# Stationary columns of the row-maximum matmuls in an LSH attention and gMLP kernel: step four against step two in the long phase

## The chip, the cores and the metric

The kernel runs on one core of a Trainium2 chip. The metric is the device time of one execution in microseconds (us); less is better. Of the kernel before there are three timed runs, and one more execution that was profiled.

## The reference

Attention with hashed buckets, for 4 batches of 8 heads, 768 positions and 64 values per head, and behind it a gated MLP on the joined heads:

```python
q_bits = (np.einsum('bhsd,dk->bhsk', q, proj) > 0)      # 6 bits make a bucket; k_bits alike
mask = q_bucket[:, :, :, None] == k_bucket[:, :, None, :]
scores = np.where(mask, scale * np.matmul(q, k.transpose(0, 1, 3, 2)), -1e9)
scores = scores - np.max(scores, axis=-1, keepdims=True)
attn = np.exp(scores)
attn = attn / (np.sum(attn, axis=-1, keepdims=True) + 1e-09)
x = np.matmul(attn, v)              # heads joined: (4, 768, 512)
h = gelu(x @ w_in); u, v = halves of h; v_n = layer norm of v
v_s = np.einsum('ts,bsd->btd', w_sg, v_n) + b_sg[None, :, None]
return x + (u * v_s) @ w_out
```

## The kernel before, in words

**Attention.** Two heads of a batch make a pair; there are 16 pairs (NPAIR). The two heads lie on partitions 0 to 63 and 64 to 127 (`row(j)`, j = 0 and 1), so most matmuls come in twos that use the two halves of the array's rows. Per pair the kernel loads q, k and v, transposes q and k on TensorE (L512), splits them into a rounded part `h` and a rest `l`, and builds a feature tile `f` (L532 and L537) whose product with itself is zero where the buckets agree and a huge negative number where not. Row MROW of each half of `f` is spare: the negated row maximum of each query is written there, so that the same product also takes the maximum away.

The 768 query columns are worked in two phases, `PHASES = ((0, 256), (256, 768))`: a short one of 256 columns (two tiles of 128 queries) and a long one of 512 columns (four tiles).

*Maxima* (`largest`, L542 to 570). A pair has 9 units, u = 0 to 8, three for each two query tiles: u = 0 to 2 belong to the short phase, 3 to 8 to the long one. In a unit 128 query columns are the weights (the stationary operand, loaded by a LDWEIGHTS) and key columns stream against them. Units with w = 0 or 1 stream 512 key columns against one query tile: 4 matmuls (f and h, two heads each). Units with w = 2 (u = 2, 5 and 8) stream the last 256 key columns against two query tiles: 8 matmuls of 256 columns. VectorE (DVE) takes the maximum of each result (L566, L568). The two results of a unit hold two PSUM slots out of seven until DVE has read them.

A query tile is not 128 neighbouring columns. Column q0 + i0 + t + step * p is query p of tile i0 + t, with step 2 in the short phase and 4 in the long one; so the weights of the long phase are read with a step of four FP32 values, those of the short phase with a step of two.

*Shift* (`shift`, L572 to 587). Behind u = 2 and u = 8 a last reduction on DVE (L576) makes `m`, 128 partitions x (head, tile), and two DMAs (L584, one per head) carry it into row MROW of `f`. With step 4 the four values of a partition are four neighbouring columns, so one DMA of 128 pieces of 16 bytes fills all 512 columns; in the short phase the pieces have 8 bytes. The DMAs are issued by SyncE (SP), for the first pair by ScalarE (ACT). SP works its queue in order.

*Weighing* (`weigh`, L589 to 639). Per unit 16 matmuls against h, l and f (L609), with contiguous key columns as weights, exp on ACT (L614), sums over units on GpSimd (POOL, L636), and products with v (L627 short, L624 long). The first three matmul steps of a unit do not read `f`; the fourth does, and it needs the shift. `finish` (L643 to 684) adds up the sums (L658), sends them through DRAM (s, sq, r, rs: five DMAs) and writes the pair's result to `xs`.

**MLP**, per batch: `hidden` (L826, L854), `gate` (L872), `project` (L898), with weights split by DVE, ACT and POOL (`weight_job`).

**The order** is written by a planner (`Plan.order`): each group of instructions has an engine, an assumed cost, a priority (smaller is sooner) and what it reads and writes. The planner plays all engines forward with those costs and emits every engine's instructions in the order that comes out. The assumed cost of a maxima unit is 0.45 us for w below 2 and 0.48 us for w = 2, in both phases; of a POOL add 1.29 us. On TensorE a group of another form (row, col, full, c32) ranks STAY later than its priority. Weigh unit c of pair n has priority 2 * (9 n + c); maxima unit u runs AHEAD = 8 units earlier, at S0P behind that; SHIFTP is added to it for the shift; FINP is the offset of `finish`, WP that of the attention's share of weight jobs; FIRSTS and LATE space the first pairs; MLP["wg"], ["wo"] and ["x"] are the priorities of the gate weights, the output weights and the next batch's loads. A DMA with `lat` keeps its queue busy for its cost, and what it writes is due SHIFTL = 3.2 us after its start.

Of the kernel before, what the change touches and what calls it, by code (L numbers as in the profile page):

```python
# [9 lines left out]
F32 = mybir.dt.float32  # L10
# [8 lines left out]
DRAM = bass.MemoryType.DRAM  # L19


MLP = {"xl": "POOL", "gm": "DVE", "gl": "POOL", "wg": 79.89, "wo": 101.06, "x": 735.35}

AVP = 5.16
GY, GX, NPT = (1, 2), (3, 3), 16
NAV = 1
S0P = 0.64
AHEAD = 8
PREP, SHIFTP, FINP, WSTEP, WP = -3.11, 0.54, 2.09, 14.6, 13.23
LOADS = "SP"  # L30
ADDS = (["POOL", "POOL"], ["POOL", "POOL", "POOL", "POOL", "POOL"])
TAILP = 0.59
FIRSTP, FIRSTS, FIRSTQ, LATE = 1.7, 0.42, -5.0, 5.94
WHURRY = 20.0
JOBBANK = False
AHEAD1 = 0.14
# [1 line left out]
SHIFTL = 3.2  # L38


class Plan:
# [8 lines left out]
    TURNS = {"row": 0.2, "col": 0.144, "full": 0.17, "c32": 0.1, None: 0.0}  # L50
    LANES = 8
    TURN = 4.7
    STAY = 3.9

    class Buf:
        def __init__(self, make, i, prev, need=None):
# [54 lines left out]
    def order(self):  # L111
# [13 lines left out]
        free, seq, ready, dma_free, pe, till, lanes = {}, {}, {}, 0.0, {}, {}, []  # L125
# [8 lines left out]
        def when(n):  # L134

            return max([at[n]] + [sorted(b.slots.values())[i] for i, b in enumerate(wants[n])])
# [7 lines left out]
        while len(out) < len(G):  # L144

            first = {}
            for e, rs in ready.items():
                ws = [n for n in rs if wants[n]]
                if len(ws) > 1:
                    t = min(max(when(n), since(n)) for n in rs)  # L150
                    m = min((n for n in ws if max(at[n], since(n)) <= t + 1e-9), key=lambda n: (G[n]["p"], n), default=None)
                    if m is not None:
                        first[e] = m

            def early(n):
                e = G[n]["e"]
                return not wants[n] or e not in first or first[e] == n

            t0, e = min((max(when(n), since(n)), e) for e, rs in ready.items() for n in rs if early(n))
            if t0 > 1e8:  # L160
                raise RuntimeError("no slot becomes free")
            def rank(n):
                return G[n]["p"] + (self.STAY if e == "PE" and G[n]["form"] != form else 0.0), n

            n = min((n for n in ready[e] if early(n) and max(when(n), since(n)) <= t0 + 1e-9), key=rank)
            g = G[n]
            soon = [m for m in ready[e] if early(m) and max(when(m), since(m)) <= t0 + self.SOON * g["c"] and rank(m) < rank(n)]
            if soon:
                n = min(soon, key=rank)
                g = G[n]  # L170
            ready[e].remove(n)
            start = max(t0, when(n), since(n))
            cost = g["c"]
            if e == "PE":

                work = g["c"] + (self.TURNS[g["form"]] if g["form"] != form else 0.0)
                form = g["form"]
                at_, cost = start, 0.0
                while work > 1e-9:

                    k = int(at_ / self.TICK + 1e-9)
                    slow = 2.0 if pe.get(k - 1, 0.0) < self.WARM * self.TICK else 1.0
                    t = min(work * slow, (k + 1) * self.TICK - at_)
                    pe[k] = pe.get(k, 0.0) + t / slow
                    work, at_, cost = work - t / slow, at_ + t, cost + t
            end, seq[e] = start + cost, start
            if g["dma"] and g["c"] > 1 and not g["lat"]:
                end = dma_free = max(dma_free, start + 0.6) + self.TURN
                seq[e] = max(start + 3.6, end - 1.5)
                end += 0.3  # L190
                lanes.append(end + self.WAIT)
            elif g["lat"]:

                seq[e], end = end, start + g["lat"]
                lanes.extend([end + self.WAIT] * (2 if g["c"] > 1 else 1))
            elif g["dma"]:
                seq[e] = end
                end = dma_free = max(dma_free, start + (1.38 if e == "ACT" else 1.3 if g["c"] > 1 else 1.2)) + g["dma"]
                end += 0.75
                lanes.append(end + self.WAIT)  # L200
            else:
                free[e] = end
                if g["port"]:
                    port = end
            out.append((start, n))
            at_end[n] = end
            for b in wants[n]:
                b.i = min(b.slots, key=b.slots.get)
                b.slots[b.i] = 1e9
            for b in g["slots"]:  # L210
                left[b] -= 1
                till[b] = max(till.get(b, 0), end)
                if not left[b]:
                    b.slots[b.i] = till[b] + self.WAIT
            for m in users[n]:
                need[m] -= 1
                if n in G[m]["deps"]:
                    at[m] = max(at[m], end if G[m]["e"] == e and not g["dma"] else end + self.WAIT)
                else:
                    at[m] = max(at[m], start)  # L220
                if not need[m]:
                    ready[G[m]["e"]].append(m)
# [12 lines left out]
def kernel(  # L235
# [19 lines left out]
    P = 128  # L255
# [42 lines left out]
    BL, MROW = 64, 0  # L298
# [94 lines left out]
    PE, DVE, ACT, POOL, SP = "PE", "DVE", "ACT", "POOL", "SP"  # L393
    xs = [[dram.tile([P, S], F32, name=f"xs_{b}_{hp}") for hp in range(NP)] for b in range(B)]

    plan = Plan()
# [45 lines left out]
    if True:  # L442
# [30 lines left out]
        def row(j):  # L473
            return slice(j * D, (j + 1) * D)

        def two(t):
            return t[:, :WIDE].rearrange("p (a b) -> p a b", a=2)
# [64 lines left out]
        def largest(st, u, prio):  # L542

            ph = 0 if u < 3 else 1
            i, w = divmod(u - 3 * ph, 3)
            if u in (0, 3):
                st.mx = plan.buf("mx", 3, lambda i: mxs[i % 3])
            mx, sc, i0 = st.mx, [ps_tile() for j in range(2)], 2 * i
            (a, b), (q0, q1) = ((0, WIDE) if w < 2 else (WIDE, S)), PHASES[ph]
            step = (q1 - q0) // P  # L550
            tiles = (w,) if w < 2 else (0, 1)

            def mm():
                for c, t in enumerate(tiles):
                    qs = slice(q0 + i0 + t, q1, step)
                    for n, x in enumerate((st.ft, st.hi)):
                        for j in range(2):
                            nc.tensor.matmul(sc[j]()[:, c * NY:c * NY + b - a], x()[row(j), 0, qs], x()[row(j), 1, a:b],  # L558
                                             start=(n == 0), stop=(n == 1))

            plan.add(PE, 0.45 if w < 2 else 0.48, prio, mm, [(x, (0, ph)) for x in (st.hi, st.ft)] + [(x, (1, c)) for x in (st.hi, st.ft) for c in ((0, 1) if w < 2 else (1,))],
                     sc, form="row")
            for j in range(2):
                def top(j=j):
                    if w < 2:
                        nc.vector.tensor_reduce(mx()[:, 0, i0 + w, j:j + 1], sc[j]()[:, :WIDE], axis=AX.X, op=ALU.max, negate=True)  # L566
                    else:
                        nc.vector.tensor_reduce(mx()[:, 1, i0:i0 + 2, j], two(sc[j]()), axis=AX.X, op=ALU.max, negate=True)  # L568

                plan.add(DVE, 0.69, prio, top, [sc[j]], [(mx, (u, j))])  # L570

        def shift(st, ph, prio):  # L572

            mx, m = st.mx, late.ring([P, 2, WIDE // P], F32R, "m", 3)
            nt = (PHASES[ph][1] - PHASES[ph][0]) // P
            plan.add(DVE, 0.18, prio, lambda: nc.vector.tensor_reduce(  # L576
                m()[:, :, :nt], mx()[:, :, :nt].rearrange("p a i j -> p j i a"), axis=AX.X, op=ALU.min), [mx], [m])
            ft, cs = st.ft, slice(*PHASES[ph])

            def carry():  # L580
                eng = nc.scalar if st.n == 0 else nc.sync
                for j in range(2):
                    r = j * BL + MROW
                    eng.dma_start(ft()[r:r + 1, 0, cs].bitcast(F32).rearrange("a (p t) -> a p t", t=nt),  # L584
                                  m()[:, j, :nt].bitcast(F32))

            plan.add(ACT if st.n == 0 else SP, 1.14, prio, carry, [m], [(ft, (0, ph))], dma=0.1, lat=SHIFTL)

        def weigh(st, c, prio):  # L589

# [108 lines left out]
        def maxima(i, p0=None):  # L699
# [3 lines left out]
            if p0 is None:  # L703
                p0 = 2 * (i - AHEAD) + S0P
            largest(sts[n], u, p0)
# [6 lines left out]
        for n in range(NPAIR):  # L712
            for c in range(NU):
                if c == 0:
                    prepare(n + 1)
                g = NU * n + c
# [8 lines left out]

    M_ = MLP
    end = even.close(early.close())
    b1 = Pool("b1", "right", None, end)
    end = odd.close(end)
    b2 = Pool("b2", "right", None, end)  # L730
    end = late.close(end)
    b3 = Pool("b3", "right", None, end)
    end = ps_s.close()
    pm = Pool("pm", "right", PSUM, end)
    end = ps_t.close(end)
# [176 lines left out]
    for b in range(B):  # L912
        p = 500 + 1000 * b
        h = hidden(b, xx, p)
# [40 lines left out]
```

## Time and profile before

| | us |
|---|---|
| median of 3 runs | 782.47 |
| lowest and highest | 781.77, 783.87 |
| the profiled execution | 784.53 |
| its span, first to last instruction | 782.7 |
| TensorE busy in the span | 766.3 (98%) |
| VectorE, ScalarE, GpSimd busy | 487.1, 330.0, 398.8 |
| granted TensorE clock, mean | 0.993 of full |

The profiled execution's own time is 784.53 us: 1.8 us lie around its span, and it is 2.06 us (0.26%) above the median. Attention takes the first 460 us, the MLP the rest; a pair takes some 27 us. Matmuls overlap, and the ends that the trace gives are modelled, so for TensorE starts are read rather than durations.

### The profile page before, as it was taken

The page shows a single profiled execution, that of the slowest core. Times are in us where ns is not written, and L with a number is a line of the kernel's source. Part 1 is how long each engine was busy: PE and PEld are TensorE (multiplying, and loading weights), DVE is VectorE, ACT ScalarE, POOL GpSimd, SP SyncE. Part 2 cuts the span into 40 slices and gives each one's busy share as a digit, 9 for nine tenths or more (in the row PEclk, how much of TensorE's full clock was granted, in tenths as well). Part 3 has the DMA queues.
Part 4 walks back from the last instruction along what each step waited for, and adds up shares of the span by engine and source line. Part 5 has one row for each costly group of instructions (what it writes and reads, how often), then busy time and mean ns, then how long its engine had stood idle before and what let it go on. Part 6 is the DMA issues. An engine that isn't in the chain of part 4 may idle for free.

```text
span 782.7 us, 14498 instructions
## 1 busy us (share of the span) xinstructions
PE 766.3 (98%) x5512; PEld 606.6 (78%) x5512; DVE 487.1 (62%) x899; ACT 330.0 (42%) x639; POOL 398.8 (51%) x366
## 2 busy tenths in 40 slices
PE   5999999999999999999999989999999999999998
PEld 4767767667676766767677549998899889988996
DVE  5897787878877899987977318688314061306130
ACT  1355555646455564545546634513332143113211
POOL 0276686768768677776877972442125023402030
PEclk9999999999999999999999989999999999999999
DMA  5223333243323323332322245411321401050003
GB/s 121 56 62 72 74 99 90 60 102 90 83 72 103 90 65 84 90 96 69 90 56 57 65 133 161 147 34 37 118 83 42 157 6 41 0 159 4 1 1 134
DMA packets 107749, 60.72 MB, mean 78 GB/s; under 512 B 73888, under 2 KB 94496, under 8 KB 107680
## 3 DMA queue, kind: packets, MB, share of 16 engines
q1 hardware_dynamic: 103840, 56.65, 26.8%
q10 hardware_dynamic: 3840, 3.16, 1.3%
q8 instruction: 43, 0.70, 0.4%
q14 instruction: 26, 0.21, 0.1%
HBM read 46.90 MB, written 12.78 MB: 76 GB/s over the span
## 4 chain that ended last, share of the span: by engine, by line
PE 94%; POOL 1%; issue 1%; DMA 1%; DVE 1%; ACTq 0%; ACT 0%; SPq 0%; POOLq 0%
PE g L609 17%; PE ps_vs L872 13%; PE g L558 10%; PE av L624 10%; PE ps_h L826 9%; PE ps_h L854 9%; PE ps_o L898 8%; PE av L627 5%; PE g L532 5%; PE g L512 3%; PE g L658 2%; PE ps_o L903 1%; POOL sum L636 1%; DMA k<-in_k_dram 1%; PE ps_h L792 1%
## 5 line engine op out<-in xcount | busy, mean ns | idle before, releaser
L636 POOL TENSOR_TENSOR sum<-sum,p 128x512 f32<-128x512 f32 x160 | 190.7, 1221 | 49.3 <-ACT p L614 49.2
L614 ACT ACTIVATE p<-g 128x512 f32<-128x512 f32 x288 | 157.7, 598 | 128.9 <-PE g L609 128.0
L566 DVE TENSOR_REDUCE mx<-g 128x1 f32<-128x512 f32 x192 | 123.4, 682 | 33.9 <-PE g L558 31.0
L636 POOL TENSOR_TENSOR sum<-p,p 128x512 f32<-128x512 f32 x64 | 83.1, 1320 | 90.9 <-ACT p L614 90.9
L624 PE MATMUL av<-p,v 128*64 128x512 f32 x384 | 89.0, 600 | 0.0
L875 DVE SCALAR_TENSOR_TENSOR gt<-ps_vs,g_col,b_bc 128x384 f32<-128x384 f32 x32 | 19.7, 616 | 92.7 <-PE ps_vs L872 90.9
L558 PE MATMUL g<-f 64*128 64x512 f32 (+1 forms) x384 | 77.0, 386 | 0.3 <-DVE mx L566 0.3
L558 PE MATMUL g<-h 64*128 64x512 f32 (+1 forms) x384 | 74.3, 373 | 0.0
L609 PE MATMUL g<-h 64*128 64x256 f32 (+1 forms) x384 | 71.6, 354 | 0.1
L883 POOL TENSOR_TENSOR gs<-gt,gs 128x384 fp32r<-128x384 f32 x32 | 32.6, 1018 | 74.9 <-ACT gs L880 74.9
L568 DVE TENSOR_REDUCE mx<-g 128x2 f32<-128x512 f32 x96 | 61.8, 683 | 13.1 <-PE g L558 12.3
L558 PEld LDWEIGHTS g<-f 64*128 64x128 f32 x384 | 55.8, 271 | 16.9 <-issue 10.3
L609 PE MATMUL g<-h,l 64*128 64x256 f32 (+1 forms) x384 | 68.4, 338 | 0.0
L609 PE MATMUL g<-f 64*128 64x256 f32 (+1 forms) x384 | 68.1, 337 | 0.0
L609 PE MATMUL g<-l,h 64*128 64x256 f32 (+1 forms) x384 | 67.8, 335 | 0.0
L898 PE MATMUL ps_o<-woh,gs 128*128 128x512 f32 x192 | 65.5, 402 | 0.0
L872 PE MATMUL ps_vs<-wgh,zh 128*128 128x384 f32 x192 | 64.1, 334 | 0.0
L872 PE MATMUL ps_vs<-wgh,zl 128*128 128x384 f32 x192 | 64.1, 334 | 0.0
L872 PE MATMUL ps_vs<-wgl,zh 128*128 128x384 f32 x192 | 64.1, 334 | 0.0
L624 PEld LDWEIGHTS av<-p,v 128*64 128x64 f32 x384 | 24.9, 136 | 46.0 <-issue 45.3
L837 POOL TENSOR_TENSOR mv<-mv,epsr 128x1 f32<-128x1 f32 x24 | 15.7, 656 | 87.6 <-DVE mv L836 87.6
L761 POOL TENSOR_TENSOR xl<-x,xh 128x768 fp32r<-128x768 f32 x16 | 29.9, 1883 | 55.1 <-ACT xh L763 55.0
(115 smaller groups left out, 1630.8 us busy)
## 6 DMA issues: line engine op xcount, KB each, us to landing
q<-in_q_dram SPq DMA_DIRECT2D x32, 192.0 KB, 3.6
v<-in_v_dram SPq DMA_DIRECT2D x16, 384.0 KB, 3.3
x<-xs SPq DMA_DIRECT2D x16, 384.0 KB, 3.0
rx<-xs SPq DMA_DIRECT2D x96, 64.0 KB, 2.0
out_dram<-ob SPq DMA_DIRECT2D x24, 256.0 KB, 2.2
k<-in_k_dram SPq DMA_DIRECT2D x30, 192.0 KB, 3.2
w<-in_moe_w_in_dram SPq DMA_DIRECT2D x16, 256.0 KB, 3.5
rs<-r SPq DMA_DIRECT2D x32, 128.0 KB, 3.0
```

The lines of the kernel that those rows point to most:

```text
L532: nc.tensor.matmul(fp()[:, c * n:(c + 1) * n], w[:, s, :], x()[:, s, cs], start=(u == 0), stop=(u == 2))
L558: nc.tensor.matmul(sc[j]()[:, c * NY:c * NY + b - a], x()[row(j), 0, qs], x()[row(j), 1, a:b], start=(n == 0), stop=(n == 1))
L566: nc.vector.tensor_reduce(mx()[:, 0, i0 + w, j:j + 1], sc[j]()[:, :WIDE], axis=AX.X, op=ALU.max, negate=True)
L568: nc.vector.tensor_reduce(mx()[:, 1, i0:i0 + 2, j], two(sc[j]()), axis=AX.X, op=ALU.max, negate=True)
L609: nc.tensor.matmul(sc[j]()[:, i * w:(i + 1) * w], x()[row(j), 1, ks], y()[row(j), 0, cs], start=(m == 0), stop=(m == 3))
L614: plan.add(ACT, 0.6, prio, lambda j=j: nc.scalar.activation(p[j]()[:, :, :NY], two(sc[j]()), AF.Exp, scale=SCALE), [sc[j]], [p[j]])
L624: nc.tensor.matmul(two(av())[row(j)], st.v()[:, j, x, :], ps[x][j]()[:, :, :NY], start=(x == 0), stop=(x == 5))
L636: (nc.gpsimd if e == POOL else nc.vector).tensor_add(two(sums[j]()), a, p[j]()[:, :, :NY])
L826: nc.tensor.matmul(ps(), x()[:, ts_], w[:, c, FH:FF], start=(c == 0 and n == 0), stop=(c == NC - 1 and n == 2))
L854: nc.tensor.matmul(ps()[:, :SH], w[:, c, fs], x()[:, cs], start=(c == 0 and n == 0), stop=(c == NC - 1 and n == 2))
L872: nc.tensor.matmul(vp(), z()[:, t, fs], w()[:, t, cs], start=(t == 0 and n == 0), stop=(t == NT - 1 and n == 2))
L898: nc.tensor.matmul(po(), a()[:, ts_], w()[:, f, :], start=(f == 0 and n == 0), stop=False)
```

## The change

The weights of a query tile in the long phase step over two columns instead of four: each two tiles (i0 and i0 + 1) share a block of 256 columns and alternate in it. The short phase is as it was. So that the maxima still reach their columns, the shift of the long phase goes in four DMAs instead of two: for each block of 256 columns and each head one DMA of 128 pieces of 8 bytes. The short phase's shift stays at two. The planner is told of the longer issue (0.57 us per DMA) and of four DMAs in flight. Ten planner numbers change as well.

```diff
-MLP = {"xl": "POOL", "gm": "DVE", "gl": "POOL", "wg": 79.89, "wo": 101.06, "x": 735.35}
+MLP = {"xl": "POOL", "gm": "DVE", "gl": "POOL", "wg": 72.25, "wo": 104.87, "x": 755.39}
-S0P = 0.64
+S0P = 0.66
-PREP, SHIFTP, FINP, WSTEP, WP = -3.11, 0.54, 2.09, 14.6, 13.23
+PREP, SHIFTP, FINP, WSTEP, WP = -3.11, 1.68, 0.2, 14.6, 14.91
-FIRSTP, FIRSTS, FIRSTQ, LATE = 1.7, 0.42, -5.0, 5.94
+FIRSTP, FIRSTS, FIRSTQ, LATE = 1.7, 0.26, -5.0, 5.43
-    STAY = 3.9
+    STAY = 4.85
...
-                lanes.extend([end + self.WAIT] * (2 if g["c"] > 1 else 1))
+                lanes.extend([end + self.WAIT] * max(1, round(g["c"] / 0.57)))
...
-            step = (q1 - q0) // P
...
-                    qs = slice(q0 + i0 + t, q1, step)
+                    qs = slice(q0 + i0 * P + t, q0 + (i0 + 2) * P, 2)
...
-                for j in range(2):
-                    r = j * BL + MROW
-                    eng.dma_start(ft()[r:r + 1, 0, cs].bitcast(F32).rearrange("a (p t) -> a p t", t=nt),
-                                  m()[:, j, :nt].bitcast(F32))
-
-            plan.add(ACT if st.n == 0 else SP, 1.14, prio, carry, [m], [(ft, (0, ph))], dma=0.1, lat=SHIFTL)
+                for h in range(0, nt, 2):
+                    hs = slice(cs.start + h * P, cs.start + (h + 2) * P)
+                    for j in range(2):
+                        r = j * BL + MROW
+                        eng.dma_start(ft()[r:r + 1, 0, hs].bitcast(F32).rearrange("a (p t) -> a p t", t=2),
+                                      m()[:, j, h:h + 2].bitcast(F32))
+
+            plan.add(ACT if st.n == 0 else SP, 0.57 * nt, prio, carry, [m], [(ft, (0, ph))], dma=0.1, lat=SHIFTL)
```

## Rows read from the trace of the kernel before

**Rows 1.** Busy time of TensorE, VectorE, ScalarE and GpSimd in three stretches (the attention's steady part, the handover to the MLP, the MLP); columns: stretch, its length, then busy us and instructions of each engine, granted clock, DMA share and GB/s.
```profile
27.00:430.00 403.00, 402.92 (x3548) 286.08 (x3548) 335.50 (x565) 213.49 (x427) 288.41 (x249) 1.00 0.32 80
430.00:460.50 30.50, 26.67 (x198) 13.68 (x199) 8.33 (x17) 15.92 (x32) 28.62 (x25) 0.98 0.27 76
460.50:782.70 322.20, 318.58 (x1663) 291.44 (x1663) 126.17 (x256) 95.13 (x173) 80.76 (x80) 0.99 0.23 73
```

**Rows 2.** Waits of TensorE's matmuls over the whole span, all there are: who waited for whom, us in total, times, longest.
```profile
PE g L512 <- DMA q<-in_q_dram: 3.3, 1, 3.3
PE g L512 <- DMA k<-in_k_dram: 3.2, 1, 3.2
PE ps_h L826 <- POOL xl L761: 2.5, 2, 2.0
PE ftp L431 <- DVE frow L328: 2.1, 1, 2.1
PE g L658 <- POOL sum L636: 1.3, 2, 0.8
PE g L558 <- DVE mx L566: 0.3, 1, 0.3
```

**Rows 3.** Weight loads by group, whole span: line, engine, operation, tiles, shape, count, busy us, mean ns of one, idle time before.
```profile
L558 PEld LDWEIGHTS g<-h 64*128 64x128 f32 x384 | 56.1, 274 | 0.5
...
L609 PEld LDWEIGHTS g<-h,l 64*128 64x128 f32 x384 | 38.8, 187 | 2.8
```

**Rows 4.** The maxima's line in two short stretches: 327.0 to 328.3 us, which holds one w = 2 unit of the long phase, and 333.9 to 336.2 us, which holds a w = 1 and a w = 2 unit of the short phase; durations in ns, least, median and most.
```profile
L558 PEld LDWEIGHTS g<-h x4: 326/326/326, 327.3 to 327.9; 64*128 64x128 f32 x4
...
L558 PEld LDWEIGHTS g<-h x6: 190/194/195, 334.1 to 335.7; 64*128 64x128 f32 x6
```

**Rows 5.** TensorE's instructions in order of time: start, us, what, count. First the four steps of a w = 2 unit of the long phase and the step behind them, then the same of the short phase.
```profile
53.21 0.39 PE L558 MATMUL g<-f 64*128 64x256 f32 x2
53.44 0.40 PE L558 MATMUL g<-h 64*128 64x256 f32 x2
53.67 0.40 PE L558 MATMUL g<-f 64*128 64x256 f32 x2
53.91 0.40 PE L558 MATMUL g<-h 64*128 64x256 f32 x2
54.14 0.28 PE L609 MATMUL g<-h 64*128 64x256 f32 x2
...
335.50 0.28 PE L558 MATMUL g<-f 64*128 64x256 f32 x2
335.62 0.28 PE L558 MATMUL g<-h 64*128 64x256 f32 x2
335.74 0.28 PE L558 MATMUL g<-f 64*128 64x256 f32 x2
335.86 0.28 PE L558 MATMUL g<-h 64*128 64x256 f32 x2
```

**Rows 6.** The chain of work that ended last, one pair's stretch from 409 us on: start, us, what, count. An x8 of L558 is a w = 2 unit, an x4 one of the others.
```profile
409.06 0.93 PE g L558 x8
...
410.95 0.46 PE g L558 x4
...
415.66 0.69 PE g L558 x4
...
417.27 0.47 PE g L558 x8
...
422.32 0.78 PE g L558 x4
...
425.43 0.82 PE g L558 x8
```

**Rows 7.** The shift's DMAs on SP and their time from issue to landing in us, from the views of that line and of DMA issues (which gives KB and the median landing).
```profile
DMA to landing us min/median/max: 1.9/1.9/3.5
```
```profile
f<-m SPq DMA_DIRECT2D x30, 1.0 KB, 1.9
f<-m SPq DMA_DIRECT2D x30, 2.0 KB, 1.9
```

**Rows 8.** In order of time: SP's issue of one long phase's shift, and TensorE's first step behind it that reads `f`.
```profile
329.90 1.17 SPq L584 DMA_DIRECT2D f<-m  x2
```
```profile
335.27 0.40 PE L609 MATMUL g<-f 64*128 64x512 f32 x2
```

**Rows 9.** SP's own waits, whole span: what the queue stood at, us in total, times, longest.
```profile
SPq L487 <- PE g L512: 52.9, 16, 8.8
```

**Rows 10.** VectorE's fullest stretches of 20 us in the attention (columns as in the first group), and its reductions of the w = 2 units (count, busy us, mean ns, idle before).
```profile
280.00:300.00 20.00, 20.00 (x176) 14.84 (x173) 18.37 (x31) 10.23 (x21) 13.55 (x12) 1.00 0.44 107
400.00:420.00 20.00, 20.00 (x168) 13.50 (x168) 18.43 (x32) 11.13 (x22) 16.30 (x15) 1.00 0.17 49
```
```profile
L568 DVE TENSOR_REDUCE mx<-g 128x2 f32<-128x512 f32 x88 | 56.7, 684 | 12.5 <-PE g L558 11.7
```

**Rows 11.** The chain at the start, and GpSimd's row at the handover with its idle time in brackets.
```profile
19.16 1.20 DVE mx L568 x2
...
21.20 1.21 PE g L558 x6
```
```profile
438.08 2.51 POOL L636 TENSOR_TENSOR sum<-p,p 128x512 f32<-128x512 f32 x2 [1.88 <-ACT p L614]
```

**Rows 12.** GpSimd's adds by group (count, busy us, mean ns), and the output weights' last step with the line that reads them (least, median and most ns, first and last start).
```profile
L636 POOL TENSOR_TENSOR sum<-sum,p 128x512 f32<-128x512 f32 x160 | 190.7, 1221 | 49.3 <-ACT p L614 49.2
```
```profile
L898 PE MATMUL ps_o<-wol,gs x96: 387/389/398, 549.5 to 778.0; 128*128 128x512 f32 x96
L387 DVE SCALAR_TENSOR_TENSOR wol<-owx,woh x8: 416/417/424, 492.4 to 546.6; 128x256 fp32r<-128x256 f32 x8
```

## The prediction

> **What bounds the kernel now.** I began with busy time by stretch, since the change lies in the attention alone. From 27 to 430 us TensorE is busy for 402.92 of 403.00 us at the full granted clock; VectorE has 335.50 us there, GpSimd 288.41 and ScalarE 213.49 [rows 1]. The reader is to see that one engine has no gap and the others have a sixth or more. The waits agree: of all that TensorE's matmuls waited for, 0.3 us fell on the maxima (L558) and nothing on the shift [rows 2]. So in the steady attention a microsecond that TensorE does not need is a microsecond of the result, as long as the others keep up. From 430 to 460.5 us it is otherwise: GpSimd is busy for 28.62 of 30.50 us [rows 1], and TensorE's speed counts for little. The MLP behind it is TensorE's again (318.58 of 322.20 us), with no line that the edit of the weights touches.
>
> The third view was the weight loads. Those of the maxima take 274 ns on average, those of the weighing, of the same shape, 187 ns [rows 3]. The average hides two kinds, and two short stretches part them: in a unit of the long phase each load takes 326 ns, in the short phase 190 to 195 ns [rows 4]. Both load 64 x 128 values; what differs is the step, four columns against two. **Step two costs as good as nothing over contiguous weights, step four about 130 ns per load.**
>
> Whether that reaches the time is read from starts. A step here is a load and a matmul for each of the two heads. In a w = 2 unit of the long phase steps start at 53.21, 53.44, 53.67, 53.91 and 54.14 us: 0.23 us each. In the short phase, with the same 256 streamed columns, at 335.50, 335.62, 335.74 and 335.86: 0.12 us [rows 5]. So w = 2 units of the long phase are held by their loads. Units with w = 0 or 1 stream 512 columns, and the chain gives such a unit of the long phase 0.46 us for two steps, 0.23 each [rows 6], the same as the rate at which strided loads come: there the load is just covered, and step two gains nothing.
>
> **Part 1, the weights.** In the chain a long w = 2 unit takes 0.93 us among 256-column steps and 0.82 us among 512-column ones, where its first load hides under the longer step before; a short one takes 0.47 us [rows 6]. Every pair has one of each kind in the long phase (u = 8 and u = 5). The gain per pair is (0.93 - 0.47) + (0.82 - 0.47) = 0.46 + 0.35 = 0.81 us. Fifteen pairs' worth lies in the steady part, where TensorE has no gap: 15 x 0.81 = 12.15 us.
>
> A smaller gain lies where a strided load stands behind a turn to another form, with no matmul to hide under: the long unit behind L658 takes 0.78 us, the short one behind L624 0.69 [rows 6], so about 0.1 us. How many of these places the new order keeps is open: 0 to one per pair, 16 x 0.1 = 1.6 us; I take half of the pairs, 0.7 us.
>
> The remaining pair's worth lies in the first 22 us, where the chain runs over VectorE's reductions (1.20 us for one unit) and over six matmuls of a maxima unit that take 1.21 us [rows 11]. At best the unit shrinks as in the steady part, at worst VectorE holds it anyway: 0 to 0.81 us, and I take 0.6, nearer to the upper end, since the chain there passes from VectorE back to the matmuls.
>
> Sum of part 1: 12.15 + 0.7 + 0.6 = 13.45 us, rounded to **13.5 us**.
>
> The Trainium skill speaks against this part: "TensorE: Matmul & The Clock Gate", section on LDWEIGHTS, lets the time of a load go by its columns alone, so that the step would be free and the gain zero. It also has the other rule: "SBUF — State Buffer", section "Door 1", says that a read wants two values out of each 16-byte line, which a step of two FP32 values gives and a step of four does not. The trace's 326 against 190 to 195 ns at equal columns [rows 4] decides for the second.
>
> **Part 2, four DMAs instead of two.** SP issues two more per pair in the long phase; the present two take 1.17 us [rows 8], so the last one leaves some 1.15 us later. Its landing time should be that of the short phase's, which has the same 8-byte pieces in 1.0 KB: 1.9 us, like the 2.0 KB ones [rows 7]. Cover: the present issue begins at 329.90, the second of the two at about 330.5, landed by 332.4, and the first step that reads `f` starts at 335.27 [rows 8]: 2.9 us to spare, 1.7 after the change. With the slowest landing, 3.5 us [rows 7], 1.3 us to spare become 0.1. The distance is TensorE's own work between u = 8 and the long phase, which part 1 does not shorten. So I cost it at nothing; without the cover it would be 1.15 us per pair, 17 us in all. What stands behind it on SP is the chain of `finish` (s, sq, r, rs, xs) and the raw loads, late by 1.15 us, which no TensorE wait of the steady part shows [rows 2]. In the first pair the issue is ACT's, same size.
>
> The skill's "DMA: Bandwidth & Descriptors", rules for kernel authors, advises against splitting small transfers, as each carries about 2 us of fixed cost. An estimate from it, if these costs came one behind the other: 4 us more per shift, beyond the cover. The equal 1.9 us of both sizes [rows 7] shows the fixed part, and the 0.6 us between issues that the parts overlap.
>
> **Part 3, the planner's numbers.** The assumed 0.48 us for w = 2 was wrong by 0.34 to 0.45 us in the long phase and becomes right (0.47), so order and machine agree better. SHIFTP lets the shift's reduction and DMAs rank 1.14 later, still ahead of the next pair's first maxima (2.0 later); it may fall behind other VectorE work of one reduction, 0.68 us [rows 10], inside the 1.7 us of cover. FINP moves `finish`, its L658 matmuls and its DMAs, up by about one unit, past the shift's issue on SP and GpSimd's adds. It may not be placed ahead of its sums in the plan, as an add is assumed at 1.29 us and measures 1.22 [rows 12]; TensorE now waits 1.3 us in two of these [rows 2]. STAY makes turns of form rarer or moves them; a turn costs about 0.2 us (0.69 against 0.46 for the same unit [rows 6]), so one turn per pair more or less is 3 us either way. I take zero. The wo number puts the output weights behind part of the gate's VectorE work; the last is ready at about 547.0 and first read at 549.5 [rows 12], and the next batch's hidden layer can fill in. wg and x pass no other priority: zero. The handover can gain at most GpSimd's 1.88 us of idle time [rows 11], or lose as much; zero.
>
> **Sum.** 784.53 - 13.5 = 771.0 us against the profiled execution's own time. That execution is 2.06 us above the median of the runs, so I forecast 782.47 - 13.5 = **769.0 us**. Own range of this case: 3 us for turns and 2 us for handover and start do not add up in one direction as a rule; 764.5 to 773.5.
>
> **Rivals.**
>
> *A. VectorE gives half of it back.* Its 335.50 us in a stretch that shrinks to about 390 us make 86%; its fullest stretches, 18.37 and 18.43 of 20 us [rows 10], come to 95%. A faster w = 2 unit asks for two reductions of 0.68 us as before, and its PSUM slots come free no sooner. Against it: the maxima's waits are VectorE's on TensorE (11.7 us before L568 [rows 10]), hardly the reverse. If every second unit's gain returns as a wait for a slot: 782.47 - 6.7 = 775.7 us. Chance 0.09.
>
> *B. Slower: the shift comes late.* SP works in order. Its raw loads (L487) stand for TensorE's transposes 16 times, 3.3 us on average [rows 9]. If the new order puts a long shift behind such a load in each pair, it lands 1.15 + 3.3 = 4.45 us later, 1.55 beyond the present 2.9 us of cover; fifteen times that is 23 us: 769 + 23 = 792 us. The point from which it decides: a shift that lands 2.9 + (13.5 + 2.3) / 15 = 3.95 us later than now makes the kernel slower by more than 0.3%. For it: the shift ranks later. Against it: the planner knows SP's order, and only 1.15 us are certain. Chance 0.05.
>
> *C. No gain: the load was not the limit,* or the new weights load no faster, for instance because the place in the tile and not the step sets the speed. Then 782.5 us. Against it stands the short phase in the same trace. Chance 0.04.
>
> *D. More:* the new order saves a turn per pair (3 us), some of GpSimd's idle time (1.9 us) and the upper bounds of part 1 (1.1 us): 763 us. Chance 0.06.
>
> **How the numbers follow.** The forecast's chance is 0.76. The range 763.5 to 775.0 us takes in nearly all of it, about half of D and some of A, 0.8 in all. About 0.3% (2.3 us) is what a measurement of this kernel can tell from no change. Faster by more: forecast, A and D, 0.91. Within: C, 0.04. Slower: B, 0.05.
>
> **What would show it.** Right: loads of L558 at 190 to 195 ns in both phases, mean near 190 instead of 274; x8 pieces of the chain at 0.47 us throughout; x4 pieces unchanged at 0.46; a pair about 0.8 us shorter; four L584 issues in 2.3 us, landing 1.9 us; still no TensorE wait for `f`. The MLP's stretch within 2 us of its 322.20. Wrong: new waits of TensorE on VectorE's maxima (A), or gaps ahead of the first f step of a long phase with the shift's DMA as releaser (B), or loads still above 300 ns (C). The sum fails most easily in part 3, whose terms are set to zero between bounds.

## The result

The changed kernel takes **768.61 us** (median of four runs, 768.24 to 768.78) against 782.38 for the kernel before beside it: ratio 0.9821, 95% interval 0.9804 to 0.9838, or 13.8 us less. The forecast was 769.0. A second comparison, told with the last experiments on the planner, gave 770.04 against 781.86 us: ratio 0.9842 (0.9819 to 0.9865), 11.8 us less.

The profiled execution took 768.58 us, its span 766.8. That is 15.9 us below the span before, more than between the medians. Part of the surplus is the clock: the page's slices of the granted clock show a dip at the handover before and none after. There the granted clock was 0.50, the 1.2 GHz level, from 459.4 to 466.2 us, and fell while TensorE waited 2.04 us for GpSimd's `xl`; after, it was 1.00, 2.4 GHz, in every stretch. The first line is the kernel before, the second the changed one.

```profile
PEclk9999999999999999999999989999999999999999
```
```profile
PEclk9999999999999999999999999999999999999999
```

Busy time of TensorE, VectorE, ScalarE and GpSimd of the changed kernel in the stretches that answer to [rows 1], moved forward by what had been gained:

```profile
27.00:417.00 390.00, 389.65 (x3560) 267.06 (x3558) 337.52 (x567) 214.32 (x426) 291.56 (x250) 1.00 0.33 82
417.00:447.00 30.00, 26.44 (x183) 13.60 (x182) 10.78 (x14) 15.53 (x31) 28.67 (x24) 1.00 0.28 82
447.00:766.80 319.80, 314.78 (x1657) 287.91 (x1655) 125.75 (x256) 94.39 (x172) 80.47 (x79) 1.00 0.23 73
```

TensorE does about the same instructions of the attention in 13 us less and still has no gap. VectorE's 337.52 us are now 86.5% of the stretch, 83% before. Handover and MLP look much as they did. The MLP's 319.80 us here hang on where the stretch was cut; from TensorE's first step of the hidden layer behind the attention (456.04 us before, 440.93 after) to the end it is 326.7 us before and 325.9 after.

The weight loads, by group over the whole span (the answer to [rows 3]), and for one long w = 2 unit alone (to [rows 4]):

```profile
L557 PEld LDWEIGHTS g<-h 64*128 64x128 f32 x384 | 39.7, 192 | 2.2
...
L610 PEld LDWEIGHTS g<-h,l 64*128 64x128 f32 x384 | 38.1, 185 | 2.9
```
```profile
L557 PEld LDWEIGHTS g<-h x4: 192/192/193, 51.5 to 51.8; 64*128 64x128 f32 x4
```

All loads of the maxima now take 192 ns; the 326 ns of the long phase are gone. The steps of that unit in order of time (start, us, what), which answer to the first half of [rows 5]:

```profile
51.53 0.28 PE L557 MATMUL g<-f 64*128 64x256 f32 x2
51.65 0.29 PE L557 MATMUL g<-h 64*128 64x256 f32 x2
51.77 0.29 PE L557 MATMUL g<-f 64*128 64x256 f32 x2
51.89 0.29 PE L557 MATMUL g<-h 64*128 64x256 f32 x2
52.01 0.29 PE L610 MATMUL g<-h 64*128 64x256 f32 x2
```

0.12 us a step instead of 0.23. The chain of the same pair as in [rows 6]; the x8 pieces are u = 8, u = 2 and u = 5:

```profile
395.97 0.48 PE g L557 x8
...
397.41 0.46 PE g L557 x4
...
402.12 0.68 PE g L557 x4
403.72 0.47 PE g L557 x8
...
408.44 0.67 PE g L557 x3
...
411.41 0.47 PE g L557 x8
```

The two long ones are down from 0.93 and 0.82 us to 0.47 and 0.48, the x4 piece stays at 0.46. The piece behind a turn, 0.78 before, is 0.67, but with three matmuls on the chain instead of four; by TensorE's starts that unit takes 0.69 us before and 0.58 after. The first of these units starts 13.1 us earlier than its counterpart, the last 14.0.

The shift in the tightest pair, and in an ordinary one: SP's issues, then TensorE's first steps that read `f` (the answers to [rows 8]); the landing times; and what one issue takes on SP (least, median and most ns), before and after:

```profile
134.12 3.67 SPq L585 DMA_DIRECT2D f<-m  x4
...
186.82 2.47 SPq L585 DMA_DIRECT2D f<-m  x4
```
```profile
139.41 0.41 PE L610 MATMUL g<-f 64*128 64x512 f32 x2
...
192.12 0.40 PE L610 MATMUL g<-f 64*128 64x512 f32 x2
```
```profile
f<-m SPq DMA_DIRECT2D x90, 1.0 KB, 1.9
```
```profile
L584 SPq DMA_DIRECT2D f<-m x60: 482/532/657, 39.1 to 433.1; - x60
```
```profile
L585 SPq DMA_DIRECT2D f<-m x90: 481/551/1797, 38.7 to 419.6; - x90
```

In the ordinary pair the four issues end at 189.29, the last began 0.56 us before and landed by 190.68: 1.4 us ahead of its reader. In the tight pair shown the third issue took 1.8 us; the last began at 137.24, landed at 139.17 after the usual 1.9 us, and its reader starts at 139.41: 0.2 us to spare. One other pair is as tight, for the same reason. With two transfers no issue took more than 0.66 us; why some take 1.0 to 1.8 us with four is open. TensorE's waits name no such transfer; these are all those of the maxima and of weighing on VectorE:

```profile
PE g L610 <- DVE mx L565: 0.5, 2, 0.4
PE g L557 <- DVE f L537: 0.4, 1, 0.4
PE g L557 <- DVE mx L565: 0.4, 1, 0.4
```

### The profile page after: what moved, and what is told of

Read it like the earlier page. It is cut to its first block, busy times and chain, and to the rows that moved or that the text cites. A ratio compares the mean times of both kernels' runs of the same rounds, so it can differ in the third digit from the quotient of the medians.

```text
span 766.8 us, 14586 instructions
## 1 busy us (share of the span) xinstructions
PE 748.0 (98%) x5512; PEld 581.7 (76%) x5512; DVE 492.1 (64%) x899; ACT 331.3 (43%) x639; POOL 402.6 (53%) x366
## 4 chain that ended last, share of the span: by engine, by line
PE 92%; DVE 2%; POOL 2%; DMA 1%; issue 1%; ACT 0%; ACTq 0%; DVEq 0%; POOLq 0%
PE g L610 17%; PE ps_vs L873 13%; PE av L625 11%; PE g L557 9%; PE ps_h L855 9%; PE ps_o L899 9%; PE ps_h L827 8%; PE av L628 5%; PE g L532 5%; PE g L512 3%; PE g L659 2%; PE ps_o L904 1%; DMA k<-in_k_dram 1%; POOL sum L637 1%; PE ps_h L793 1%
## 5 line engine op out<-in xcount | busy, mean ns | idle before, releaser
L557 PE MATMUL g<-f 64*128 64x512 f32 (+1 forms) x384 | 69.7, 356 | 1.0 <-DVE f L537 0.4
L610 PE MATMUL g<-h 64*128 64x256 f32 (+1 forms) x384 | 69.9, 346 | 0.5 <-DVE mx L565 0.5
L557 PE MATMUL g<-h 64*128 64x512 f32 (+1 forms) x384 | 65.3, 336 | 0.0
L557 PEld LDWEIGHTS g<-f 64*128 64x128 f32 x384 | 40.1, 192 | 23.3 <-issue 17.4
```

Of the source, the lines that this page charges most:

```text
L610: nc.tensor.matmul(sc[j]()[:, i * w:(i + 1) * w], x()[row(j), 1, ks], y()[row(j), 0, cs], start=(m == 0), stop=(m == 3))
```

## The experiments

The theory: the loads of the long phase's w = 2 units are the gain, the added transfers hide, the planner's numbers are worth nothing. The rivals: the order that the numbers make carries a good part; the transfers cost part.

**Only the step taken back.** The changed kernel with the weights at step four; the transfers stay four, each of 8-byte pieces that land 16 bytes apart. The order of every engine is that of the changed kernel.

```diff
-                    qs = slice(q0 + i0 * P + t, q0 + (i0 + 2) * P, 2)
+                    qs = slice(q0 + i0 + t, q1, (q1 - q0) // P)
...
-                        eng.dma_start(ft()[r:r + 1, 0, hs].bitcast(F32).rearrange("a (p t) -> a p t", t=2),
+                        eng.dma_start(ft()[r:r + 1, 0, cs].bitcast(F32).rearrange("a (p t) -> a p t", t=nt)[:, :, h:h + 2],
```

> The changed kernel, every engine's order unchanged, four transfers of 8-byte pieces in the long phase, but the weights at step four again (the pieces land 16 bytes apart). Only the step of the weights differs from the changed kernel. Theory: 768.6 + 13.5 = 782 us, within 2, x8 pieces at 0.82 to 0.94 us. Rival (the place of the columns or the order, not the step): 770 us or less.

Measured: 783.23 us, ratio to before 1.0011 (1.0001 to 1.0020). Its chain, at the same units:

```profile
409.30 0.94 PE g L557 x8
...
422.23 0.79 PE g L557 x4
...
425.35 0.82 PE g L557 x8
```

The step alone is worth 783.23 - 768.61 = 14.6 us in the new order (13.2 against the 770.04 of the second comparison); the number of transfers and the order have no part in that.

**Old numbers.** The changed kernel with the ten old numbers:

```diff
-MLP = {"xl": "POOL", "gm": "DVE", "gl": "POOL", "wg": 72.25, "wo": 104.87, "x": 755.39}
+MLP = {"xl": "POOL", "gm": "DVE", "gl": "POOL", "wg": 79.89, "wo": 101.06, "x": 735.35}
-S0P = 0.66
+S0P = 0.64
-PREP, SHIFTP, FINP, WSTEP, WP = -3.11, 1.68, 0.2, 14.6, 14.91
+PREP, SHIFTP, FINP, WSTEP, WP = -3.11, 0.54, 2.09, 14.6, 13.23
-FIRSTP, FIRSTS, FIRSTQ, LATE = 1.7, 0.26, -5.0, 5.43
+FIRSTP, FIRSTS, FIRSTQ, LATE = 1.7, 0.42, -5.0, 5.94
-    STAY = 4.85
+    STAY = 3.9
```

> The changed weights and the four transfers with all ten planner numbers as before. Theory (the load rate of the long phase's w = 2 units is the gain, the numbers are worth nothing): 769 us, within 2, and the chain's x8 pieces of the maxima at 0.47 us. Rival (the numbers carry a good part of the gain): 774 us or more, with the x8 pieces at 0.47 us all the same and new gaps elsewhere on TensorE.

Measured: 773.7 us, ratio 0.9886 (0.9872 to 0.9901). Between the two: 5.1 us above the changed kernel, near the rival's bound, with x8 pieces of 0.47 to 0.48 us. Here the theory did not hold; the next two runs take it apart.

**New numbers alone.** The same five lines turned round, on the kernel before, and nothing else; for instance

```diff
-    STAY = 3.9
+    STAY = 4.85
```

> The kernel before with the ten new planner numbers alone: weights at step four, two transfers. TensorE's order comes out as in the changed kernel. Theory: 782 us, within 3, loads of the long phase still at 305 to 330 ns. Rival (the order is what pays): 776 us or less.

Measured: 783.68 us against 782.21, ratio 1.0017 (1.0006 to 1.0029). On the old weights the numbers bring nothing, so they have no gain of their own that could explain the 5.1 us. Their loss of 1.5 us is hardly in the steady attention: in the profiles thirteen pairs from its middle take 356.0 us against 355.7. It goes with the clock, whose mean was 0.993 to 0.996 in all ten executions, and 0.997 or more in fourteen of the nineteen of the kernel before.

**Old order.** In the run with old numbers one more thing differs from the kernel before: the planner is told that the long shift's issue takes 2.28 us and four DMAs. Take that away, and the order of TensorE, VectorE and GpSimd is the kernel before's, instruction for instruction, with the new weights and four transfers in it:

```diff
-            plan.add(ACT if st.n == 0 else SP, 0.57 * nt, prio, carry, [m], [(ft, (0, ph))], dma=0.1, lat=SHIFTL)
+            plan.add(ACT if st.n == 0 else SP, 1.14, prio, carry, [m], [(ft, (0, ph))], dma=0.1, lat=SHIFTL)
...
-                lanes.extend([end + self.WAIT] * max(1, round(g["c"] / 0.57)))
+                lanes.extend([end + self.WAIT] * (2 if g["c"] > 1 else 1))
```

> The changed weights and the four transfers, old numbers, and the planner told nothing of the longer issue, so that TensorE, VectorE and GpSimd keep the order of the kernel before instruction for instruction: the prediction's parts 1 and 2 with part 3 at exactly zero. Theory (the loads give 13.5 us in an unchanged order, the added transfers hide; the run with the old numbers lost because the longer issue made the planner choose more turns of form): 769 us, within 1.5, 131 turns in the thirteen middle pairs as before. Rival (the old order cannot take the gain, since the shift then comes late): 773 us or more, with new gaps at the first f step of the long phases.

Measured: 769.58 us, ratio 0.9836 (0.9817 to 0.9855). With an unchanged order the loads give 12.6 us (10.8 in the repeat further down). So the 4.1 us between this and the run with old numbers (2.6 against the repeat) come from the order that the planner wrote when it was told of the longer issue.

That order changes form more often. Counted in the sequence of TensorE's rows between the starts of the second and the fifteenth pair (a pair starts with its first weighing matmul), form changes 148 times with the told cost and old numbers, 131 times in the old order and 134 in the changed kernel; that stretch takes 349.5, 345.1 and 344.3 us. With the told cost 17 steps more lead from one form to another, and 17 fewer stay within a form. Summed from start to start, the steps across a turn take 46.55 us against 41.83 in the old order, the others 302.96 against 303.23. So the 4.4 us lie at the turns: 0.26 us a turn, as a mean over turns of different kinds. The number of turns does not order all runs: the changed kernel has three more than the old order and is 0.8 us shorter, its turns taking 1.4 us more and its other steps 2.2 us less.

**Told or not told, with new numbers**, beside the changed kernel and the old order on one chip. The edit is the one above, on the changed kernel.

> The changed kernel with the ten new numbers, but the planner told of an issue of 1.14 us and two transfers in the long phase, as before; four are issued all the same. TensorE's order is that of the changed kernel, VectorE's and SP's differ a little. With the run of the old order it completes the four cases of old or new numbers, told or not told. Theory (the numbers are worth about 1 us by themselves; the told issue cost matters only with the old numbers, where it adds turns): 768.6 us, within 1. Rival (the numbers were needed because the shift would come late without the told issue): 771 us or more, with waits on the shift's transfer.

> The old order with the changed weights and four transfers once more, on the same chip as the run beside it, for the difference between old and new numbers. Theory (numbers worth 1 us or less): 0.3 to 1.5 us above the run with the new numbers. Rival (worth nothing): within 0.3 us of it.

> The changed kernel itself on the same chip as the two beside it: 768.6 us, within 0.8, by either theory; it is the yardstick for the other two.

Measured: 771.59 (770.40 to 772.48), 771.09 (770.18 to 772.27) and 770.04 us (768.40 to 771.27). These are the run not told, the old order and the changed kernel. The changed kernel itself came out 0.6 us above its expected bound; its two executions at a mean clock of 0.998 and 1.000 took 768.40 and 769.50 us, the two at 0.993 and 0.995 took 770.58 and 771.27. The run not told is above the theory's bound and past the rival's 771, but its median lies 1.6 us from the changed kernel's with overlapping ranges, and the wait that the rival rests on, for a shift's transfer, does not appear among TensorE's. So neither holds as stated. The old order is 1.05 us above the changed kernel, as in the first comparison (769.58 against 768.61), also with overlapping ranges. In the profiles the thirteen middle pairs take 344.2, 345.5 and 345.6 us (changed, not told, old order); of the 1.2 us of the run not told 0.4 and 0.8 lie in two single pairs, the others are equal. A lead of the changed kernel of about 1 us is likely, but the runs do not part it from nothing. The new numbers without the told cost are no better than the old order (771.59 against 771.09).

**Half of the shift left out.** The two transfers for the second block of 256 columns are not issued, so those queries' scores keep their maximum; TensorE, VectorE and GpSimd keep their order.

```diff
-                for h in range(0, nt, 2):
+                for h in range(0, 2, 2):
```

> The changed kernel with the two transfers for the second block of 256 columns left out, so that those queries' scores keep their maximum; the orders of TensorE, VectorE and GpSimd are the same. Theory (the two added transfers are hidden): 768.6 us, within 0.8. Rival (the transfers cost part of the gain): faster by 1.5 us or more, most of it as gaps that go from the first steps of the long phases.

Measured: 769.77 us (768.33 to 770.09), ratio 0.9832 (0.9816 to 0.9849). That is 0.4 us past the theory's bound, on the side away from the rival: 1.2 us above the changed kernel's first figure, 0.3 us below the 770.04 just given. The thirteen middle pairs take 344.0 us, 344.3 in the changed kernel. The two added transfers are hidden.

**Eight transfers**, each of half the partitions, to find where the cover ends:

```diff
+                        for s in range(0, P, P * 2 // nt):
+                            e = s + P * 2 // nt
...
-                                      m()[:, j, h:h + 2].bitcast(F32))
+                                          m()[s:e, j, h:h + 2].bitcast(F32))
```

> The changed kernel with the long phase's shift in eight transfers of 64 pieces instead of four of 128, every other engine's order unchanged. The last issue leaves about 2.3 us later. In the changed kernel's trace the last issue stands 2.2 to 3.6 us ahead of the step that reads it and lands in 1.9 to 2.0, so 0.2 to 1.6 us are to spare. Theory (TensorE waits for what goes beyond the cover): about 1 us in each of some 14 pairs, 780 us, within 4. Rival (the cover is larger than it looks, for instance because steps move): within 2 us of 768.6.

Measured: 790.57 us, ratio 1.0106 (1.0079 to 1.0132), slower than before. The direction is the theory's, the size is not: 22 us, not 11 to 12. TensorE in order of time in one pair:

```profile
227.55 0.40 PE L612 MATMUL g<-l,h 64*128 64x512 f32 x2
227.78 0.39 PE L612 MATMUL g<-f 64*128 64x512 f32 x1
228.78 0.47 PE L612 MATMUL g<-f 64*128 64x512 f32 x1 [0.62 <-DMA f<-m]
228.79 0.39 PE L557 MATMUL g<-f 64*128 64x256 f32 x1
```

A unit of the long phase has 8 matmuls in four steps (16 only in the short phase), and the fourth step reads `f`. The first head's f step goes at 227.78; the second head's, due some 0.02 us later, stands until its transfer has landed, at 228.78. That is the 1 us expected, and the rows behind show single matmuls where there were twos.

The pairs tell where the rest comes from, each against the same pair of the changed kernel. In nine of the thirteen middle pairs the second head starts 0.94 to 1.08 us late and the pair is 0.99 to 1.10 us longer: the delay and hardly more. Two others have a late head of 1.5 and 1.7 us and lose 1.6 and 1.8: one of the issues ahead took 1.2 to 1.3 us instead of 0.6. Over all thirteen the head is 1.18 us late and a pair 1.46 us longer (363.2 us against 344.3). Most of what the delay leaves open lies in the other two pairs: one has a wait of 1.6 us on VectorE's maxima, the other, with an issue of 1.7 us, a granted clock of 0.50 (1.2 GHz) from 395.4 to 398.8 us, TensorE having been busy for 13.7 of the 15.4 us before. Another 3 us come from the other pairs and the handover. SP's issues in this run (ns, as above):

```profile
L587 SPq DMA_DIRECT2D f<-m x150: 475/587/1687, 39.1 to 443.0; - x150
```

**Contiguous weights.** Step one, which needs a transfer per tile and head, eight in the long phase and four in the short one:

```diff
-                    qs = slice(q0 + i0 * P + t, q0 + (i0 + 2) * P, 2)
+                    qs = slice(q0 + (i0 + t) * P, q0 + (i0 + t + 1) * P)
...
-                for h in range(0, nt, 2):
-                    hs = slice(cs.start + h * P, cs.start + (h + 2) * P)
+                for h in range(nt):
+                    hs = slice(cs.start + h * P, cs.start + (h + 1) * P)
```

> The changed kernel with contiguous weights in the long phase (step one), which asks for eight transfers, one for each tile and head, of 128 pieces of 4 bytes; every other engine's order unchanged. It is to be compared with the run of eight transfers at step two. Theory (step two already loads at the full rate): loads of 187 to 195 ns, and the time of the run with eight transfers, within 1.5 us. Rival (each step costs): loads clearly shorter than at step two and at least 2 us faster than that run.

Measured: 799.17 us, ratio 1.0217 (1.0187 to 1.0248): 8.6 us slower than the run with eight transfers, not equal to it. The times compare transfers, though, not loads. Issues and median landing, first here, then in the run with eight transfers at step two:

```profile
f<-m SPq DMA_DIRECT2D x180, 0.5 KB, 2.0
```
```profile
f<-m SPq DMA_DIRECT2D x120, 0.5 KB, 1.8
```

The transfers land 0.2 us later, and the f steps wait for them: over the thirteen middle pairs the second head is 1.5 us late in the mean, against 1.2 with eight transfers at step two. The loads are told by their own rows, step one and then step two:

```profile
L557 PEld LDWEIGHTS g<-h 64*128 64x128 f32 x384 | 42.2, 187 | 2.3
```
```profile
L557 PEld LDWEIGHTS g<-h 64*128 64x128 f32 x384 | 43.5, 192 | 1.8
```

And a long w = 2 unit at step one:

```profile
224.85 0.28 PE L557 MATMUL g<-f 64*128 64x256 f32 x2
224.97 0.28 PE L557 MATMUL g<-h 64*128 64x256 f32 x2
225.09 0.28 PE L557 MATMUL g<-f 64*128 64x256 f32 x2
```

5 ns less per load, and the same 0.12 us a step. There is nothing behind step two for these units. Of the 7.9 us between the two profiled spans 3.3 lie in the middle pairs (366.5 and 363.2) and as much between the fifteenth pair's start and the last weighing unit. In this last part the contiguous run's granted clock was 0.50 (1.2 GHz) from 429.2 to 432.6 us, TensorE having been busy for 7.7 of the 9.2 us before; the other run's was 1.00 there. The rest is open.

## Why the prediction was right, step by step

**The bound** held: TensorE without a gap in the attention, before and after, so its time was the kernel's.

**Part 1** was the gain, and its size was right. Predicted were 0.81 us a pair and about 0.7 us in all behind turns. In the unchanged order the thirteen middle pairs went from 355.7 to 345.1 us, 0.82 us a pair (345.6 and 0.78 in the repeat). In the new order (step four against step two) they went from 356.4 to 344.3 us, 0.93 a pair: such a unit behind a turn takes 0.70 us at step four and 0.57 at step two by its starts, and the new order has 13 of these places in 14 pairs, the old order 5. So the term for turns, taken for half of the pairs, holds in the new order for nearly all. That units of 512 columns gain nothing was right (x4 pieces at 0.46 us in both). The rule of the Trainium skill's "SBUF — State Buffer", section "Door 1", that two values of a 16-byte line are wanted, agrees at all three steps: 326 ns at four, 192 at two, 187 at one. That the line, and not the step by itself, sets the time is not shown; no run has a step of three.

**Part 2**, no cost, was right: without the two added transfers the middle pairs take 344.0 us, with them 344.3. Its reserve was 1.7 us at the usual landing forecast and 1.4 in the ordinary pair of the changed kernel. The 0.1 us forecast for the slowest landing came near the measured 0.2 by luck: the tight pairs come from slow issues on SP, which the forecast of 2.3 us for four did not have (2.47 us in the ordinary pair, 3.67 in the tight one), and not from a slow landing. Rival B's mechanism is real (eight transfers are slower than the kernel before), and its price, one microsecond lost for one of delay, is about what the nine ordinary pairs of that run show.

**Part 3**, zero, was right in its sum and wrong in its make-up. What it did not see: telling the planner of the longer issue was taken as harmless, while with the old numbers it costs 4.1 us (2.6 against the repeat), in the middle pairs at turns of form. With the told cost the new numbers give that back; without it they are worth nothing that the runs show, on the old weights (783.68 against 782.21) or the new (771.59 against 771.09). That cost and return cancel was not reasoned, so the hit to 0.4 us is in part luck, and the second comparison's 770.04 lies 1.0 us off. Had the numbers been left as they were, the kernel would have come out at 773.7 us, 4.7 us from the forecast: inside the last range (763.5 to 775.0) and just outside the one of the sum (764.5 to 773.5). The text's price of a turn, 0.2 us, measured 0.26; its bound of one turn more or less per pair was a little short of what the told cost brought with the old numbers, 17 in 13 pairs. Which of the ten numbers does it was not tried.

**Handover and MLP** were set to zero. By TensorE's starts 15.1 of the profiled 15.9 us were gained by the first step of the hidden layer, 0.3 of them behind the attention's last product, and 0.8 us in the MLP, which holds the clock dip before. By this measure the sign given for the MLP, within 2 us, held.

Rivals A and C did not happen: TensorE's maxima and weighing wait 1.3 us in all on VectorE's rows, and no load of the maxima takes more than 199 ns. D's saved turns did not come (134 against 131).

## What to carry to other kernels

Read the weight loads apart by access pattern before trusting a mean: 274 ns hid 190 to 195 and 326, and the strided ones cost time only where the streamed part was too short to cover them, 256 columns and not 512, or where they stood behind a turn of form. A layout that makes one engine's reads cheap is paid for in the transfers that must follow it; count the cover between the last issue and the first reader, with the slowest issue in it, since past the cover a microsecond of delay cost about a microsecond. When a planner is told a truer cost, its other numbers may no longer fit: compare in an unchanged order to see what the edit itself is worth.

## What was not expected of the hardware

With two transfers per shift no issue on SP took more than 0.66 us; with four and with eight most still took 0.5 to 0.6, but some took 1.0 to 1.8, and these made the tightest pairs. The cause is open. Of two transfers of 0.5 KB, the one of 128 pieces of 4 bytes landed in 2.0 us, the one of 64 pieces of 8 bytes in 1.8.
